# Five feature pairs of the last layer computed with seven half-width block products, and 1 + exp moved to ACT

## The chip, the core and the metric

The kernel runs on one core of a Trainium2 chip. The metric is the device time of one execution in microseconds (us). A core has TensorE (PE in the profile: matrix products; PEld is its loading of the stationary operand), VectorE (DVE), ScalarE (ACT), GpSimd (POOL) and SyncE (SP, which here issues the loads and stores). Each engine works through its own queue in order and waits for the others by semaphores.

## What is computed

The reference is attention over a window of 128 tokens plus 4 sinks, then a gated layer, then a layer with softplus. Only the last one is touched:

```python
def _moe2_ref(x, w_in, w_out):           # x: 1536 x 512, w_in: 512 x 2048, w_out: 2048 x 512
    h = x @ w_in
    g = np.maximum(h, 0.0) + np.log1p(np.exp(-np.abs(h)))
    return (g @ w_out).astype(np.float32)
```

## The kernel before

Every number that goes into a product is held as two parts, a rounded one (hi) and the rest (lo). A product of two such numbers is three matmuls, hi by hi, hi by lo and lo by hi; the helper `mm3` (lines 164 to 168) issues them, so nearly every matmul of the profile has line L166, L167 or L168.

The program has attention, two stages of the gated layer, `stage3` (which leaves the layer's input in 4 slots for each chunk of tokens, named y in the profile and `self.x2` in the code) and `stage4`, the last layer. `stage4` runs over 3 chunks `t` of 512 tokens, and in each over 16 feature blocks `f` of 128 features (called features below; features 2p and 2p+1 are pair p). One turn of the loop does this:

- 12 matmuls of 512 columns give `h` of this feature (4 blocks of 128 inputs by three matmuls) in a PSUM tile of tag `S`; there are 4 such tiles.
- `softplus` works in three steps, between which the loop does other things. First step: absolute value (ACT, L704), exp (ACT, L705), 1 + exp (POOL, L706), all into spa and spu. Second: logarithm (ACT, L709, into spl), and three steps of DVE (L711, L714, L717) that build the maximum and a correction and add them to the logarithm. Third: the hi part by a copy (ACT, L720, into gh) and the lo part by a subtraction (DVE, L151, into gl).
- The third step of a feature is issued in the next turn, behind the first step of the next feature (`next(last[2])`).
- "Value products": `outs` multiplies gh and gl of an earlier feature by `w_out`, 4 groups of 3 matmuls of 512 columns, into the four accumulators ox and o (tags X0, X1, PT). `todo` holds the features whose value products are still owed. In turn f those of feature f - 2 are issued, behind `h` of f. A feature takes 24 matmuls in all.

In chunk 0 the loop also decodes the last four blocks of weights on ACT and DVE (lines 193 to 226), and there a scheduler may move instructions. In chunks 1 and 2 (`tc.manual_schedule()`) each engine gets its instructions in the order in which the code is written. `store` copies an accumulator to SBUF and stores it. At the end the value products of three features and the last one stay behind `h`.

Of the kernel before, what the change touches and what calls it, by code (L numbers as in the profile page):

```python
# [9 lines left out]
F32 = mybir.dt.float32  # L10
FR = mybir.dt.float32r
# [25 lines left out]
NC = DM // P  # L37
NF = FF // P
NF2 = FF2 // P
CH = 512  # L40
NCH = NT // CH
MASKED = 8.0e9
SCALE = 0.125

SLOT_X = 0
# [13 lines left out]
    C=(-143.56, -520.69, 38.35, -348.75, -150.48, -361.46), T=(85.26, 85.11, 83.1, 84.82, 88.43, 82.09),  # L59
    P=(-697.11, -455.77, -631.6, -474.64, -647.58, -395.71), PV=(97.88, 94.31, 94.22, 97.88, 97.88, 169.98),  # L60
# [81 lines left out]
class Net:  # L142
# [545 lines left out]
    def softplus(self, pool, ps, f, t, parts=1):  # L688

        nc = self.nc  # L690

        def tl(n, dt=F32, nb=2):
            return pool.tile([P, CH], dt, tag=n, name=f"{n}{t}_{f}", bufs=nb)

        a, u, l = tl("spa"), tl("spu"), tl("spl")
        if (t, f) == (NCH - 1, NF2 - 1):

            g = self.slot(SLOT_AB, "glast")
            gh, gl = g[:, 0, :], g[:, 1, :]
        else:  # L700
            gh, gl = tl("gh", FR, 3), tl("gl", FR, 3)
        cuts = [slice(j * CH // parts, (j + 1) * CH // parts) for j in range(parts)]
        for c in cuts:
            nc.scalar.activation(a[:, c], ps[:, c], AF.Abs)  # L704
            nc.scalar.activation(a[:, c], a[:, c], AF.Exp, scale=-1.0)  # L705
            nc.gpsimd.tensor_scalar(out=u[:, c], in0=a[:, c], scalar1=1.0, scalar2=1.0, op0=ALU.add, op1=ALU.mult)  # L706
        yield
        for c in cuts:
            nc.scalar.activation(l[:, c], u[:, c], AF.Ln)  # L709

            nc.vector.scalar_tensor_tensor(  # L711
                out=u[:, c], in0=u[:, c], scalar=1.0, in1=a[:, c], op0=ALU.subtract, op1=ALU.subtract
            )
            nc.vector.scalar_tensor_tensor(  # L714
                out=u[:, c], in0=ps[:, c], scalar=0.0, in1=u[:, c], op0=ALU.max, op1=ALU.subtract
            )
            nc.vector.tensor_tensor(out=l[:, c], in0=l[:, c], in1=u[:, c], op=ALU.add)  # L717
        yield
        for c in cuts:
            self.last_hi = nc.scalar.copy(gh[:, c], l[:, c])  # L720
            self.lo_dve(gl[:, c], l[:, c], gh[:, c])
        yield gh, gl

    def stage4(self, pool, psum):
        tc, nc = self.tc, self.nc
        acc = {}

        def outs(t, f, g, parts=range(CH // P)):
            if f == 0:
                acc[t] = [psum.tile([P, CH], F32, tag=f"X{i}", name=f"ox{t}_{i}", bufs=1) for i in range(2)]  # L730
                acc[t] += [psum.tile([P, CH], F32, tag="PT", name=f"o{t}_{i}", bufs=2) for i in range(2)]
            wh, wl = self.w4[f]
            for i in parts:
                k = slice(i * P, (i + 1) * P)
                self.mm3(acc[t][i], (g[0][:, k], g[1][:, k]), (wh[:, 1, :], wl[:, 1, :]), f == 0, f == NF2 - 1)

        def store(t, i, queue=nc.sync):
            r = t * CH + i * P
            o = self.slot(SLOT_X + t * NC + i, f"os{t}_{i}", F32)[:, 0, :]
# [4 lines left out]
            queue.dma_start(out=self.out[r : r + P, :], in_=o)  # L744

        todo, last = [], None
        for t in range(NCH):
            with tc.manual_schedule() if t else contextlib.nullcontext():
                for f in range(NF2):
                    if t == 0 and f in (3, 5, 7, 9):  # L750
                        self.w4_unit(12 + (f - 3) // 2, self.last_hi)
                    if (t, f) == (NCH - 1, NF2 // 2) and self.bad is None:
                        self.bad = self.flag_load()
                    wh, wl = self.w4[f]
                    ps = psum.tile([P, CH], F32, tag="S", name=f"h{t}_{f}", bufs=4)
                    for ct in range(NC):
                        k = slice(ct * P, (ct + 1) * P)
                        x = self.x2[t][ct]
                        self.mm3(ps, (wh[:, 0, k], wl[:, 0, k]), (x[:, 0, :], x[:, 1, :]), ct == 0, ct == NC - 1)
                    sp = self.softplus(pool, ps, f, t, 2 if (t, f) == (NCH - 1, NF2 - 1) else 1)  # L760
                    next(sp)
                    if last:
                        todo.append((*last[:2], next(last[2])))
                    next(sp)
                    last = (t, f, sp)
                    if len(todo) > (1 if (t, f) < (NCH - 1, NF2 - 2) else 3):
                        o = todo.pop(0)
                        outs(*o)
                        if o[1] == NF2 - 1:
                            for i in range(CH // P):  # L770
                                store(o[0], i)
                if t == NCH - 1:

                    while len(todo) > 1:
                        outs(*todo.pop(0))
                    before, n = todo.pop(), CH // P
                    outs(*before, parts=[0, 1])
                    g = next(last[2])
                    for i in range(n):
                        outs(t, NF2 - 1, g, parts=[i])  # L780
                        store(t, i, nc.sync if i < 2 else nc.scalar)
                        if i + 2 < n:
                            outs(*before, parts=[i + 2])


    def dense_masks(self, pool):
# [6 lines left out]
        for i in range(QT):  # L793
# [175 lines left out]
```

## Time and profile before

| | us |
|---|---|
| median of 3 runs | 583.76 (583.74 to 584.16) |
| profiled execution | 584.81 |
| its span, first to last instruction | 582.9 |
| share of the span with PE busy | 98% |
| DVE, ACT, POOL | 74%, 60%, 14% |

The profile is of one execution. A matmul's record runs from its start to the modelled end of its last result, and the next one starts earlier, so the pace of matmuls is read from their starts. Idle time of an engine that nobody waits for costs nothing.

### The profile page before, as it was taken

The page shows a single profiled execution, that of the slowest core. Times are in us where ns is not written, and L with a number is a line of the kernel's source. Part 1 is how long each engine was busy: PE and PEld are TensorE (multiplying, and loading weights), DVE is VectorE, ACT ScalarE, POOL GpSimd, SP SyncE. Part 2 cuts the span into 40 slices and gives each one's busy share as a digit, 9 for nine tenths or more (in the row PEclk, how much of TensorE's full clock was granted, in tenths as well). Part 3 has the DMA queues.
Part 4 walks back from the last instruction along what each step waited for, and adds up shares of the span by engine and source line. Part 5 has one row for each costly group of instructions (what it writes and reads, how often), then busy time and mean ns, then how long its engine had stood idle before and what let it go on. Part 6 is the DMA issues. An engine that isn't in the chain of part 4 may idle for free.

```text
span 582.9 us, 9844 instructions
## 1 busy us (share of the span) xinstructions
PE 573.5 (98%) x3718; PEld 472.8 (81%) x3718; DVE 431.0 (74%) x906; ACT 347.1 (60%) x712; POOL 82.4 (14%) x162
## 2 busy tenths in 40 slices
PE   9999999999999999999999999999999999999996
PEld 6888788888888888888888777888888888888885
DVE  6889899999989976767988889845644554654553
ACT  7999967667566754545666668544444344444352
POOL 4657700000000000000000221111111011011010
PEclk9999999999999999999999999999999999999999
DMA  7566645454445523342643221000200000200002
GB/s 275 172 221 195 188 140 149 139 151 151 133 144 148 164 88 108 114 140 72 201 128 106 74 72 37 0 1 0 73 0 2 0 1 1 73 0 1 0 1 79
DMA packets 15512, 54.51 MB, mean 94 GB/s; under 512 B 1888, under 2 KB 1888, under 8 KB 15456
## 3 DMA queue, kind: packets, MB, share of 16 engines
q1 hardware_dynamic: 15168, 53.27, 29.3%
q8 instruction: 31, 0.51, 0.4%
q10 hardware_dynamic: 288, 0.52, 0.3%
q14 instruction: 25, 0.20, 0.1%
HBM read 50.64 MB, written 3.15 MB: 92 GB/s over the span
## 4 chain that ended last, share of the span: by engine, by line
PE 86%; POOL 4%; DVE 3%; ACT 3%; issue 2%; DMA 1%; SPq 0%; POOLq 0%; DVEq 0%
PE ab L166 8%; PE ab L168 7%; PE ab L167 7%; PE h L167 6%; PE h L168 6%; PE h L166 6%; PE x2p L168 4%; PE x2p L166 4%; PE x2p L167 4%; PE ox L168 3%; PE o L167 3%; PE o L168 3%; PE o L166 3%; PE ox L167 3%; PE ox L166 3%; PE w34p L168 2%
## 5 line engine op out<-in xcount | busy, mean ns | idle before, releaser
L706 POOL TENSOR_SCALAR spu<-spa 128x512 f32<-128x512 f32 (+1 forms) x49 | 35.9, 733 | 458.7 <-ACT spa L705 458.7
L151 DVE TENSOR_TENSOR gl<-spl,gh 128x512 fp32r<-128x512 f32 x47 | 32.6, 694 | 76.8 <-ACT gh L720 76.5
L704 ACT ACTIVATE spa<-h 128x512 f32<-128x512 f32 (+1 forms) x49 | 28.7, 586 | 86.5 <-PE h L168 86.3
L166 PE MATMUL ab<-x,u_w 128*128 128x512 f32 x192 | 74.8, 390 | 0.0
L167 PE MATMUL ab<-x,u_w 128*128 128x512 f32 x192 | 74.7, 389 | 0.0
L168 PE MATMUL ab<-x,u_w 128*128 128x512 f32 x192 | 74.7, 389 | 0.0
L166 PE MATMUL h<-y,w4h 128*128 128x512 f32 x192 | 74.7, 389 | 0.0
L167 PE MATMUL h<-y,w4h 128*128 128x512 f32 x192 | 74.7, 389 | 0.0
L168 PE MATMUL h<-y,w4l 128*128 128x512 f32 x192 | 74.7, 389 | 0.0
L193 ACT ACTIVATE dt_w<-raw_w 128x512 bf16<-128x512 bf16 x64 | 42.5, 669 | 52.1 <-DMA raw_w<-w4d 16.9
L201 DVE SCALAR_TENSOR_TENSOR dc_w<-raw_w,dt_w 128x512 uint16<-128x512 uint16 x64 | 44.2, 697 | 10.1 <-ACT dt_w L196 9.6
L196 ACT ACTIVATE dt_w<-dt_w,rebias 128x512 uint16<-128x512 uint16 x64 | 45.8, 721 | 1.3
L711 DVE SCALAR_TENSOR_TENSOR spu<-spu,spa 128x512 f32<-128x512 f32 (+1 forms) x49 | 33.3, 680 | 16.6 <-ACT spl L709 16.6
L709 ACT ACTIVATE spl<-spu 128x512 f32<-128x512 f32 (+1 forms) x49 | 30.4, 623 | 24.5 <-POOL spu L706 24.5
L407 POOL TENSOR_SCALAR e<-e,st 128x196 f32<-128x196 f32 (+1 forms) x96 | 39.5, 434 | 23.4 <-ACT e L393 17.1
L393 ACT ACTIVATE e<-e,st 128x196 f32<-128x196 f32 (+1 forms) x96 | 42.2, 447 | 0.9 <-DVE st L386 0.7
L168 PEld LDWEIGHTS ab<-x,u_w 128*128 128x128 f32 x192 | 36.1, 188 | 7.5
L167 PEld LDWEIGHTS h<-y,w4h 128*128 128x128 f32 x192 | 36.1, 188 | 7.5
L167 PEld LDWEIGHTS ab<-x,u_w 128*128 128x128 f32 x192 | 36.0, 188 | 7.5
L166 PEld LDWEIGHTS h<-y,w4h 128*128 128x128 f32 x192 | 36.0, 188 | 7.5
L166 PEld LDWEIGHTS ab<-x,u_w 128*128 128x128 f32 x192 | 36.0, 188 | 7.4
L168 PEld LDWEIGHTS h<-y,w4l 128*128 128x128 f32 x192 | 36.0, 188 | 7.4
(127 smaller groups left out, 1306.4 us busy)
## 6 DMA issues: line engine op xcount, KB each, us to landing
raw_w<-w4d SPq DMA_DIRECT2D x32, 511.8 KB, 4.2
raw_w<-w SPq DMA_DIRECT2D x16, 511.8 KB, 4.6
raw_w<-w3t SPq DMA_DIRECT2D x16, 511.8 KB, 3.8
qk<-qk SPq DMA_DIRECT2D x7, 792.0 KB, 4.5
raw_wo<-wod SPq DMA_DIRECT2D x8, 511.8 KB, 3.8
v<-vu SPq DMA_DIRECT2D x8, 400.0 KB, 5.5
v<-v SPq DMA_DIRECT2D x8, 384.0 KB, 4.6
out<-os SPq DMA_DIRECT2D x10, 256.0 KB, 2.3
```

Source lines behind the costliest of these rows:

```text
L151: return engine.tensor_tensor(out=lo, in0=x, in1=hi.bitcast(F32), op=ALU.subtract)
L166: nc.tensor.matmul(ps, lhs[0], rhs[0], start=start, stop=False)
L167: nc.tensor.matmul(ps, lhs[0], rhs[1], start=False, stop=False)
L168: nc.tensor.matmul(ps, lhs[1], rhs[0], start=False, stop=stop)
L193: return nc.scalar.activation(t.bitcast(BF), x["top"].bitcast(BF), AF.Abs)
L196: return nc.scalar.activation(x["t"], x["t"], AF.Relu, bias=self.rebias[:, 0:1], scale=8.0)
L201: nc.vector.scalar_tensor_tensor(out=c, in0=x["top"], scalar=0x8000, in1=t, op0=ALU.bitwise_and, op1=ALU.bitwise_or)
L393: nc.scalar.activation(e, e, AF.Exp, bias=st[:, 0, i : i + 1], scale=-1.0, accum_out=st[:, 1, i : i + 1])
L407: nc.gpsimd.tensor_scalar(out=e, in0=e, scalar1=buf("st", h)[:, 2, i : i + 1], scalar2=1.0, op0=ALU.mult, op1=ALU.mult)
L706: nc.gpsimd.tensor_scalar(out=u[:, c], in0=a[:, c], scalar1=1.0, scalar2=1.0, op0=ALU.add, op1=ALU.mult)
L709: nc.scalar.activation(l[:, c], u[:, c], AF.Ln)
L711: nc.vector.scalar_tensor_tensor(out=u[:, c], in0=u[:, c], scalar=1.0, in1=a[:, c], op0=ALU.subtract, op1=ALU.subtract)
```

## The change

For pairs 3, 5 and 7 of chunk 1 and pairs 3 and 5 of chunk 2, `h` of the two features is no longer 24 matmuls of 512 columns. The pair is taken as a 2 x 2 by 2 x 2 block product (2 features by 2 halves of the inputs, times 2 halves of the inputs by 2 halves of the tokens), and that is formed from seven block products of sums, each of 6 matmuls of 256 columns: 42 matmuls in place of 24.

The sums are made on DVE ahead of time and split into hi and lo: for the weights once for each pair (`weight_steps`, issued in feature 2p - 2, tiles wr and ws), for the tokens twice for each chunk (`token_steps`, tiles xr and ts: in features 14 of chunk 0 and 2 of chunk 1, and in 0 and 2 of chunk 2). In `seven` DVE then adds the products into a tile `hp` in SBUF, from which `softplus` reads both features at once. The value products of the two features before the pair are cut in their 8 groups: one behind the second product, four between the sixth (the fourth of the tiles A, Bk, C, E) and the last, three behind that.

The second edit is in `softplus`: 1 + exp is an Identity with a bias on ACT. Its bias is a second column of the tile `rebias`, which gets a second memset. Chunk 0 stores through two slots in place of four.

```diff
@@ softplus
-            nc.gpsimd.tensor_scalar(out=u[:, c], in0=a[:, c], scalar1=1.0, scalar2=1.0, op0=ALU.add, op1=ALU.mult)
+            nc.scalar.activation(u[:, c], a[:, c], AF.Identity, bias=self.one[:, 0:1])
@@ stage4
+        def whole(r, hi, lo):
+            nc.vector.tensor_tensor(out=r, in0=hi.bitcast(F32), in1=lo.bitcast(F32), op=ALU.add)
+        def combine(out, x, y, op):
+            nc.vector.tensor_tensor(out=out, in0=x, in1=y, op=op)
...
+        def parts_of(r, dst):
+            for j in range(2):
+                nc.scalar.copy(dst[j][:, 0, :], r[j])
+            yield
+            for j in range(2):
+                self.lo_dve(dst[j][:, 1, :], r[j], dst[j][:, 0, :])
+            yield
...
+        def weight_steps(t, p):
+            r = pair_of_r(f"wr{t}_{p}")
+            for dst, f in zip(r, (2 * p + 1, 2 * p)):
+                hi, lo = self.w4[f]
+                whole(dst, hi[:, 0, :], lo[:, 0, :])
+            a11, a12, a21, a22 = r[0][:, HN], r[0][:, HM], r[1][:, HN], r[1][:, HM]
+            combine(a22, a21, a22, ALU.add)
+            combine(a21, a11, a21, ALU.subtract)
+            combine(a11, a22, a11, ALU.subtract)
+            combine(a12, a12, a11, ALU.subtract)
+            yield
+            self.ws = [self.slot(SLOT_X + j, f"ws{t}_{p}_{j}") for j in range(2)]
+            yield from parts_of(r, self.ws)
+        def product(ps, a, b, start=True):
+            for c in range(2):
+                self.mm3(ps, a(c), b(c), start and c == 0, c == 1, skip_group_check=True)
...
+            product(A[:, HN], part(odd, 0), tok(0, HN))
+            p1 = quarter("dt", "p1")
+            nc.scalar.copy(p1, A[:, HN])
+            before()
+            chunks = [lambda o=o, i=i: outs(*o, parts=[i]) for o in todo for i in range(CH // P)]
+            product(Bk[:, HN], part(even, 2), tsum(1, HN))
+            chunks[0]()
+            product(A[:, HN], part(odd, 2), tok(2, HN), False)
+            nc.scalar.copy(ho[:, HN], A[:, HN])
+            product(Bk[:, HM], wsum(0, 0), tsum(1, HM))
+            u2 = quarter("dc", "u2")
+            combine(u2, Bk[:, HM], p1, ALU.add)
+            product(C[:, HN], wsum(1, 0), tsum(0, HN))
+            u3 = quarter("dt", "u3")
+            combine(u3, C[:, HN], u2, ALU.add)
+            combine(he[:, HN], u3, Bk[:, HN], ALU.subtract)
+            product(E[:, HN], wsum(1, 2), tsum(0, HN))
+            combine(he[:, HM], E[:, HN], u3, ALU.add)
+            for c in chunks[1:5]:
+                c()
+            product(E[:, HN], wsum(0, 2), tok(2, HM), False)
+            combine(ho[:, HM], E[:, HN], u2, ALU.add)
+            for c in chunks[5:]:
+                c()
+            e = self.softplus(pool, he, 2 * p, t)
...
+        lots = {1: (3, 5, 7), 2: (3, 5)}
@@ the loop, around softplus of a plain feature
+                    sums = steps.get((t, f), iter(lambda: 0, 1))
+                    next(sums)
                     sp = self.softplus(pool, ps, f, t, 2 if (t, f) == (NCH - 1, NF2 - 1) else 1)
                     next(sp)
+                    next(sums)
                     if last:
                         todo.append((*last[:2], next(last[2])))
                     next(sp)
+                    next(sums)
```

The order is shown at two places of chunk 1: between pairs 3 and 5 on DVE and ACT, and at the start of pair 5 on PE. Names end in chunk and feature: h1_8 is `h` of feature 8 in chunk 1; the long numbers are buffers, and each version has its own line numbers.

**First place.** DVE before, from the end of feature 7 to that of feature 8:

```order
L717 TENSOR_TENSOR spl1_7_4771<-spl1_7_4771,spu1_7_4770 128x512
L151 TENSOR_TENSOR gl1_7_4773<-spl1_7_4771,gh1_7_4772 128x512
L711 SCALAR_TENSOR_TENSOR spu1_8_4809<-spu1_8_4809,spa1_8_4808 128x512
L714 SCALAR_TENSOR_TENSOR spu1_8_4809<-h1_8_4795,spu1_8_4809 128x512
L717 TENSOR_TENSOR spl1_8_4810<-spl1_8_4810,spu1_8_4809 128x512
L151 TENSOR_TENSOR gl1_8_4812<-spl1_8_4810,gh1_8_4811 128x512
```

The lo part of feature 7 is followed at once by the three steps of feature 8.

DVE after, the same stretch; wr are the sums of the weights of pair 5 and ws their two parts:

```order
L152 TENSOR_TENSOR gl1_7_4857<-spl1_7_4855,gh1_7_4856 128x512
L753 TENSOR_TENSOR wr1_5_0_4882<-w4h11_3744,w4l11_3745 128x512
L753 TENSOR_TENSOR wr1_5_1_4883<-w4h10_3740,w4l10_3741 128x512
L756 TENSOR_TENSOR wr1_5_1_4883<-wr1_5_1_4883 128x256
L756 TENSOR_TENSOR wr1_5_1_4883<-wr1_5_0_4882,wr1_5_1_4883 128x256
L756 TENSOR_TENSOR wr1_5_0_4882<-wr1_5_1_4883,wr1_5_0_4882 128x256
L756 TENSOR_TENSOR wr1_5_0_4882<-wr1_5_0_4882 128x256
L712 SCALAR_TENSOR_TENSOR spu1_8_4891<-spu1_8_4891,spa1_8_4890 128x512
L715 SCALAR_TENSOR_TENSOR spu1_8_4891<-h1_8_4869,spu1_8_4891 128x512
L718 TENSOR_TENSOR spl1_8_4892<-spl1_8_4892,spu1_8_4891 128x512
L152 TENSOR_TENSOR ws1_5_0_4898<-wr1_5_0_4882,ws1_5_0_4898 128x512
L152 TENSOR_TENSOR ws1_5_1_4899<-wr1_5_1_4883,ws1_5_1_4899 128x512
```

The next row is `gl1_8_4894`. So eight instructions came in: six sums between features 7 and 8, and two rests ahead of the lo part of feature 8.

ACT before, from the logarithm of feature 7 to the hi part of feature 8:

```order
L709 ACTIVATE spl1_7_4771<-spu1_7_4770 128x512
L704 ACTIVATE spa1_8_4808<-h1_8_4795 128x512
L705 ACTIVATE spa1_8_4808<-spa1_8_4808 128x512
L720 CAST gh1_7_4772<-spl1_7_4771 128x512
L709 ACTIVATE spl1_8_4810<-spu1_8_4809 128x512
L704 ACTIVATE spa1_9_4847<-h1_9_4834 128x512
L705 ACTIVATE spa1_9_4847<-spa1_9_4847 128x512
L720 CAST gh1_8_4811<-spl1_8_4810 128x512
```

The logarithm of feature 8 waits for POOL and stands behind two copies and activations of features 7 and 8 alone.

ACT after, the same stretch:

```order
L710 ACTIVATE spl1_7_4855<-spu1_7_4854 128x512
L721 CAST gh1_7_4856<-spl1_7_4855 128x512
L705 ACTIVATE spa1_8_4890<-h1_8_4869 128x512
L706 ACTIVATE spa1_8_4890<-spa1_8_4890 128x512
L707 ACTIVATE spu1_8_4891<-spa1_8_4890,rebias_60 128x512
L773 CAST ws1_5_0_4898<-wr1_5_0_4882 128x512
L773 CAST ws1_5_1_4899<-wr1_5_1_4883 128x512
L710 ACTIVATE spl1_8_4892<-spu1_8_4891 128x512
L705 ACTIVATE spa1_9_4933<-h1_9_4920 128x512
L706 ACTIVATE spa1_9_4933<-spa1_9_4933 128x512
L707 ACTIVATE spu1_9_4934<-spa1_9_4933,rebias_60 128x512
L721 CAST gh1_8_4893<-spl1_8_4892 128x512
```

The two copies of the sums stand ahead of the logarithm of feature 8, the hi part of feature 7 ahead of feature 8's absolute value, and 1 + exp is new.

**Second place.** PE before, the end of `h` of feature 10 and the first value products of feature 8:

```order
L166 MATMUL h1_10_4873<-y1_3_3512,w4h10_3739 128x512
L167 MATMUL h1_10_4873<-y1_3_3512,w4h10_3739 128x512
L168 MATMUL h1_10_4873<-y1_3_3512,w4l10_3740 128x512
L166 MATMUL ox1_0_4584<-w4h8_3731,gh1_8_4811 128x512
L167 MATMUL ox1_0_4584<-w4l8_3732,gh1_8_4811 128x512
L168 MATMUL ox1_0_4584<-w4h8_3731,gl1_8_4812 128x512
```

All 12 matmuls of feature 10 stand ahead of the value products of feature 8.

PE after, from the middle of the second product of pair 5:

```order
L167 MATMUL q1_5_1_4960<-ts1_1_1_4600,w4h10_3740 128x256
L168 MATMUL q1_5_1_4960<-ts1_1_1_4600,w4h10_3740 128x256
L169 MATMUL q1_5_1_4960<-ts1_1_1_4600,w4l10_3741 128x256
L167 MATMUL ox1_0_4611<-w4h8_3732,gh1_8_4893 128x512
L168 MATMUL ox1_0_4611<-w4l8_3733,gh1_8_4893 128x512
L169 MATMUL ox1_0_4611<-w4h8_3732,gl1_8_4894 128x512
```

Between the value products of feature 7 and the first of feature 8 stood 12 matmuls of 512 columns; now 12 of 256 stand there.

## Rows read from the trace of the kernel before

**Rows 1.** The page's head: span, busy time (share) xinstructions, clock in 40 slices.

```profile
span 582.9 us, 9844 instructions
PE 573.5 (98%) x3718; PEld 472.8 (81%) x3718; DVE 431.0 (74%) x906; ACT 347.1 (60%) x712; POOL 82.4 (14%) x162
PEclk9999999999999999999999999999999999999999
```

**Rows 2.** Stretches of the last layer: us, busy of each engine (xinstructions), clock, DMA.

```profile
314.00:397.00 83.00, 81.90 (x355) 65.91 (x354) 65.18 (x104) 50.46 (x88) 15.06 (x15) 1.00 0.10 33
397.00:482.00 85.00, 85.00 (x376) 70.41 (x375) 44.97 (x66) 37.67 (x64) 9.87 (x16) 1.00 0.04 13
```

**Rows 3.** Timeline of PE in chunk 2: start us, us, engine, line, operation, xcount.

```profile
487.01 0.39 PE L166 MATMUL h<-y,w4h 128*128 128x512 f32 x1
487.23 0.39 PE L167 MATMUL h<-y,w4h 128*128 128x512 f32 x1
...
487.69 0.39 PE L166 MATMUL ox<-w4h,gh 128*128 128x512 f32 x1
...
488.37 0.39 PE L166 MATMUL ox<-w4h,gh 128*128 128x512 f32 x1
```

**Rows 4.** Timeline, a feature's softplus in chunk 2; in brackets idle before, and releaser.

```profile
487.89 0.60 ACT L704 ACTIVATE spa<-h 128x512 f32<-128x512 f32 x1 [2.81 <-PE h L168]
488.52 0.63 ACT L705 ACTIVATE spa<-spa 128x512 f32<-128x512 f32 x1
...
490.55 0.69 DVE L711 SCALAR_TENSOR_TENSOR spu<-spu,spa 128x512 f32<-128x512 f32 x1 [0.16 <-ACT spl L709]
491.27 0.69 DVE L714 SCALAR_TENSOR_TENSOR spu<-h,spu 128x512 f32<-128x512 f32 x1
492.00 0.69 DVE L717 TENSOR_TENSOR spl<-spl,spu 128x512 f32<-128x512 f32 x1
...
494.49 0.60 ACT L720 CAST gh<-spl 128x512 fp32r<-128x512 f32 x1
495.13 0.70 DVE L151 TENSOR_TENSOR gl<-spl,gh 128x512 fp32r<-128x512 f32 x1 [2.44 <-ACT gh L720]
```

**Rows 5.** Timeline of chunk 0 around one instruction of POOL.

```profile
341.44 1.29 DVE L210 SCALAR_TENSOR_TENSOR dr_w<-raw_w,dt_w 128x512 f32<-128x512 uint32 x2
...
341.96 3.05 POOL L706 TENSOR_SCALAR spu<-spa 128x512 f32<-128x512 f32 x1 [5.72 <-ACT spa L705]
...
344.21 0.39 PE L167 MATMUL ox<-w4l,gh 128*128 128x512 f32 x1
344.59 0.50 PE L168 MATMUL ox<-w4h,gl 128*128 128x512 f32 x1
344.93 0.39 PE L166 MATMUL ox<-w4h,gh 128*128 128x512 f32 x1
...
345.05 0.63 ACT L709 ACTIVATE spl<-spu 128x512 f32<-128x512 f32 x1 [3.17 <-POOL spu L706]
```

**Rows 6.** POOL by line, in chunk 0 and in chunks 1 and 2.

```profile
L706 POOL TENSOR_SCALAR spu<-spa 128x512 f32<-128x512 f32 x15 | 15.1, 1004 | 303.3 <-ACT spa L705 303.3
L706 POOL TENSOR_SCALAR spu<-spa 128x512 f32<-128x512 f32 (+1 forms) x34 | 20.9, 614 | 155.4 <-ACT spa L705 155.4
```

**Rows 7.** Loads of weights in chunk 1, by line: busy us, mean ns.

```profile
L167 PEld LDWEIGHTS h<-y,w4h 128*128 128x128 f32 x64 | 12.0, 188 | 2.5
```

**Rows 8.** Timeline of PE in attention: short matmuls with a new weight each.

```profile
14.68 1.08 PE L420 MATMUL pt<-ident,e 128*68 128x128 f32 x8
```

**Rows 9.** DVE by line, 512 columns in chunks 1 and 2, 256 at the end.

```profile
L717 DVE TENSOR_TENSOR spl<-spl,spu 128x512 f32<-128x512 f32 x31 | 21.5, 693 | 1.1
...
L717 DVE TENSOR_TENSOR spl<-spl,spu 128x256 f32<-128x256 f32 x2 | 0.8, 424 | 0.1
```

**Rows 10.** ACT by line: plain and with a bias tile, 512 columns.

```profile
L705 ACT ACTIVATE spa<-spa 128x512 f32<-128x512 f32 x32 | 20.2, 632 | 1.0
L720 ACT CAST gh<-spl 128x512 fp32r<-128x512 f32 x31 | 18.7, 604 | 0.0
...
L196 ACT ACTIVATE dt_w<-dt_w,rebias 128x512 uint16<-128x512 uint16 x8 | 5.3, 707 | 0.0
```

**Rows 11.** DVE by line in attention, 256 columns with one input in PSUM.

```profile
L151 DVE TENSOR_TENSOR x<-xt,x 128x256 fp32r<-128x256 f32 x9 | 3.5, 408 | 0.0
```

More of the change, by code (lines that the diff above doesn't have):

```diff
@@ L41 @@
 NCH = NT // CH
+HN, HM = slice(0, CH // 2), slice(CH // 2, CH)
 MASKED = 8.0e9
@@ new lines, in pair_of_r, with token_steps @@
+        def pair_of_r(name):
+            return [self.dec.tile([P, CH], F32, tag="dr", name=f"{name}_{j}", bufs=2) for j in range(2)]
+        def parts_of(r, dst):
[5 more added lines that the diff above has]
+            yield
+        def token_steps(t, c):
+            r = pair_of_r(f"xr{t}_{c}")
+            token_sums(t, c, r)
+            yield
+            for j in range(2):
+                name = f"ts{t}_{c}_{j}"
+                if (c, j) == (1, 1):
+                    self.ts[c, j] = self.slot(SLOT_X + 3, name)
+                else:
+                    self.ts[c, j] = self.dec.tile([P, 2, CH], FR, tag="raw", name=name, bufs=3)
+            yield from parts_of(r, [self.ts[c, j] for j in range(2)])
@@ new lines, in product, with seven, part, tok @@
+        def product(ps, a, b, start=True):
+            for c in range(2):
+                self.mm3(ps, a(c), b(c), start and c == 0, c == 1, skip_group_check=True)
+        def seven(t, p, before, todo):
+            odd, even, x = self.w4[2 * p + 1], self.w4[2 * p], self.x2[t]
+            def part(pair, c0):
+                return lambda c: tuple(w[:, 0, (c0 + c) * P : (c0 + c + 1) * P] for w in pair)
+            def tok(c0, cols):
+                return lambda c: tuple(x[c0 + c][:, j, cols] for j in range(2))
+            def wsum(j, c0):
+                return lambda c: tuple(self.ws[j][:, k, (c0 + c) * P : (c0 + c + 1) * P] for k in range(2))
+            def tsum(j, cols):
+                return lambda c: tuple(self.ts[c, j][:, k, cols] for k in range(2))
+            def quarter(tag, n):
+                return self.dec.tile([P, CH // 2], F32, tag=tag, name=f"{n}_{t}_{p}", bufs=2)
+            A, Bk, C, E = [psum.tile([P, CH], F32, tag="S", name=f"q{t}_{p}_{j}", bufs=4) for j in range(4)]
+            h = self.slot(SLOT_X + 2, f"hp{t}_{p}", F32)
+            he, ho = h[:, 0, :], h[:, 1, :]
+            product(A[:, HN], part(odd, 0), tok(0, HN))
[10 more added lines that the diff above has]
+            combine(u2, Bk[:, HM], p1, ALU.add)
+            product(C[:, HN], wsum(1, 0), tsum(0, HM))
+            u3 = quarter("dt", "u3")
[10 more added lines that the diff above has]
+            e = self.softplus(pool, he, 2 * p, t)
+            next(e)
+            next(e)
+            o = self.softplus(pool, ho, 2 * p + 1, t)
+            next(o)
+            g = next(e)
+            next(o)
+            return [(t, 2 * p, g), (t, 2 * p + 1, next(o))]
@@ L746, in stage4 @@
+        self.ts, steps = {}, {}
+        lots = {1: (3, 5, 7), 2: (3, 5)}
+        steps[0, NF2 - 2], steps[1, 2] = token_steps(1, 0), token_steps(1, 1)
+        steps[2, 0], steps[2, 2] = token_steps(2, 0), token_steps(2, 1)
+        for t, lot in lots.items():
+            for p in lot:
+                steps[t, 2 * p - 2] = weight_steps(t, p)
         todo, last = [], None
         for t in range(NCH):
+            pairs = lots.get(t, ())
             with tc.manual_schedule() if t else contextlib.nullcontext():
@@ L753, in stage4, with before @@
                         self.bad = self.flag_load()
+                    if f // 2 in pairs:
+                        if f % 2 == 0:
+                            def before():
+                                todo.append((*last[:2], next(last[2])))
+                            todo = seven(t, f // 2, before, todo)
+                            last = None
+                        continue
                     wh, wl = self.w4[f]
@@ L911, in run @@
             self.val = const.tile([P, 2], F32, name="val")
-            self.rebias = const.tile([P, 1], F32, name="rebias")
+            both = const.tile([P, 2], F32, name="rebias")
+            self.rebias, self.one = both[:, 0:1], both[:, 1:2]
             self.idle = const.tile([P, P], BF, name="idle")
@@ L915, in run @@
             nc.vector.memset(self.rebias, -8.0 * 16 * 896)
+            nc.vector.memset(self.one, 1.0)
             nc.scalar.preload_act_table_set("natural_log_exp_and_others")
```

25 lines of the change are left out of this document (20 added, 5 removed).

## The prediction

> **What bounds the kernel now.** I read the page's head first: PE is busy for 98% of the span at the full granted clock, its 2.4 GHz level [rows 1]. So only what shortens or stops PE's stream counts. Then the stretches of the last layer and the starts of matmuls in it: six intervals take 488.37 - 487.01 = 1.36 us, 0.2267 each [rows 3]. In chunk 1, 376 matmuls at that pace are 85.2 us for a stretch of 85.0: PE never waits. In chunk 0, 355 are 80.5 of 83.0: 2.5 us are lost, which the busy column hides, since records overlap [rows 2] (a few records may be missing, so this is no better than to 0.5).
>
> Where they are lost shows the timeline of chunk 0: POOL's 1 + exp takes 3.05 us from 341.96, while DVE works without a pause; the logarithm has to wait for it until 345.05 [rows 5]. By line POOL's step means 1.00 us in chunk 0 and 0.61 later [rows 6]. DVE is behind by then, and PE stops for gl. A late weight also costs a restart: the matmul at 344.59 lasts 0.50 in place of 0.39 and the next starts 0.34 later, 0.11 over the pace.
>
> Last, one feature of chunk 2: the steps of ACT and DVE, with ACT idle 2.81 and DVE 2.44 in a turn of 5.44 [rows 4]. `h` of this feature ends at 487.69, gl at 495.83, and its value products come four half turns after `h`, at 498.57: 2.7 us to spare. That slack must carry the sums.
>
> **The change, part by part.**
>
> *The products.* A pair had 24 matmuls at 0.2267, 5.44 us; it gets 42 of 256 columns, whose pace the trace does not show. Bounds: half of 0.2267 is 0.113; a load of weights is on record for 0.188 [rows 7], and if it could not lie under the matmul before, that would be the pace. Loads need not be alone: eight matmuls of 128 columns with a new weight each take 1.08 us, 0.28 of it the last one's own record, so 0.114 each [rows 8]; and the restart above costs 0.11, not 0.188. At 2.4 GHz one column a cycle is 213 ns for 512, which leaves 13 per matmul; 107 + 13 = 0.120 is my value. 42 x 0.120 = 5.04, 0.40 less; five pairs: **-2.0 us** (-3.4 at 0.113, +12.3 at 0.188; even at 0.130).
>
> The Trainium skill (TensorE: Matmul & The Clock Gate, Back-to-back issue gap) gives columns over 2.4 GHz and 2.5 ns, 0.216 at 512, where the row has 0.227. By it the 256 columns would pass in 0.109 and the products alone bring -4.3 us. Which end is nearer decides one of the rivals below.
>
> *1 + exp.* POOL's step goes, and with it the waits of chunk 0 except some 0.4 at its start: **-2.1 us** (0 to -2.5). ACT takes over 16 steps there, 11 us on top of 50.5 in 83 [rows 2]; this fits. A step is 0.63 without a bias tile and 0.707 with one [rows 10]; the edit has one, so I take 0.707. In chunks 1 and 2 it replaces 0.62 and two handovers, so nobody gains. The memset is once, at the start, beside loads; the stores of chunk 0 keep their times.
>
> *The sums and the chain behind them.* Prices: a DVE step of 512 is 0.69, of 256 columns 0.42 [rows 9] (0.41 with an input in PSUM [rows 11]). If it needs the result just before, the next starts 0.035 later [rows 4], if not, 0.08 sooner: two take 1.29 [rows 5]. The sums of a pair are 0.61 + 0.73 + 4 x 0.46 = 3.17 us of DVE, two copies 1.1 of ACT, two rests 1.2 of DVE. Averaged over two pairs (21 us) DVE has room: 4 features x 2.8 + 3.2 + 1.2 + five sums in the pair 2.2 = 17.8. What matters is that the order is fixed. The order rows show the sums between gl of feature 7 and the first step of feature 8, the copies ahead of its logarithm, the rests ahead of its gl. So feature 8 waits for all that.
>
> The place is pair 5 of chunk 1. Let Z be the moment when PE leaves the seventh product of pair 3. PE then has three value groups (2.04), `h` of 8, value products of 6, `h` of 9, value products of 7 (2.72 each) and two products (1.44): it wants gh of feature 8 at **Z + 14.4**. Before, with a whole `h` in place of the two products, that was 2.72 - 1.44 = 1.3 later.
>
> DVE and ACT meanwhile, both features of pair 3 being ready almost at once and `softplus` of 7 queued behind that of 6. DVE is done with feature 5 some 3.5 before Z, four sums of products (0.46 each) end at Z - 1.7, four steps of ACT for feature 6 (0.64, 0.67, 0.74, 0.67) bring the logarithm at Z + 0.9. Then there is no pause: three DVE steps (0.73 each) to 3.1, gh 0.64 to 3.7, gl 0.61, three steps for feature 7 to 6.5, gh to 7.15, gl to 7.8, the sums 3.17 to 10.9, two copies 1.05 to 12.0, logarithm 0.66 to 12.6, three steps to 14.8, gh to 15.4, and with handover and restart (0.15) PE goes on at **Z + 15.6**. It waits 1.2. After two matmuls it wants gl; that stands behind the two rests, begins at 15.95, ends at 16.65 and restarts PE at 16.8, another 0.75. Together 2.0.
>
> The same reckoning elsewhere, each with its own start:
> - pair 7 of chunk 1 and pair 5 of chunk 2 lie alike, 2.2 each: the first begins with DVE already late, in the second ACT reads the flag of the window first;
> - pair 3, twice: sums start when DVE is through with feature 3, 0.8 after `h` of 4; 3.2 more, two copies 1.05 and gh 0.6 make 5.7 with the restart, against 5.44; gl 0.27 later. 0.5 each;
> - features 14 and 15 of chunk 1, computed at once by pair 7: 1.0;
> - sums of tokens in feature 2, twice, behind the copies to be stored: 0.3 each.
>
> Sum 2.0 + 2.2 + 2.2 + 1.0 + 1.0 + 0.6 = **+9.0 us**. Bounds: if a sum of 256 columns took 0.38, the waits would lose 2, at 0.46 they gain 2; handovers of 0.06 in place of 0.035 add 3. Without the bias tile (0.63) they lose 0.6.
>
> The Trainium skill (ScalarE: Activation LUTs, What ACT_TABLE_LOAD costs) prices an activation of 512 columns at 0.61 with an immediate bias and 0.71 with a tile's. The trace has 0.63 and 0.707: it agrees on the second. Taken at 0.61 the sum would come out 0.8 lower.
>
> Sum: -2.0 - 2.1 + 9.0 = **+4.9 us**. The profiled execution of 584.81 (582.9 span and 1.9 around it) would be 589.7. It lies 1.05 over the median of 583.76, and 583.76 + 4.9 = 588.7 is the forecast.
>
> **The rivals.**
>
> *The sums stay hidden* (the other side). Mechanism: the chain between pairs 3 and 5 ends before PE asks. It is 14.7 us from Z + 0.9 against 13.5 that PE leaves. The waits fall below the 4.1 that the rest brings when it shrinks by about 1 us, 7%. For: DVE is idle for half of chunk 1 [rows 2], and nobody saw these sums of 256 columns in such a row. Against: each step has a row of its shape. Largely hidden, the waits are 1: -2.0 - 2.1 + 1.0 = -3.1, 580.7.
>
> *The load of weights is the pace.* 0.188 per product [rows 7]: 5 x 42 x 0.068 = 14.3 more on PE. The slower products give the chain more time, 4 of the waits go: 4.9 + 14.3 - 4 = +15, 599. Against: rows 8 and the restart of 0.11. It outweighs the forecast from 0.14 on.
>
> *The edit of 1 + exp frees nothing in chunk 0.* ACT, first in the chain there, takes 0.71 for POOL's 0.62 and has the decoding to do; if the waits stay, +4.9 + 2.1 = +7.0, 590.8.
>
> *A quicker product.* If all of a matmul's time goes with its columns, 256 pass in 0.113, 5 x 42 x 0.007 = 1.5 less on PE. At the four places where the chain of DVE ends last PE only waits longer; about 0.2 remains, 588.5. The gap rule of the Trainium skill named above lies at this end: 0.109, and some 0.4 off the time.
>
> **Chances and range.** Forecast 0.66, quick product 0.08, no gain in chunk 0 0.10, load-bound 0.06, hidden 0.10, of which 0.08 end below -0.2% and 0.02 near no change; 0.02 more of the forecast's own lower tail fall within. A measurement of this kernel tells 0.2%, 1.2 us, from no change. So faster 0.08, same 0.04, slower 0.88. The range takes the prices of the sums (+2.0 to +8.5): 585.9 to 592.3. It leaves out the load-bound case, the hidden one and a few hundredths at both ends.
>
> **What would show it.** Right: starts of 256-column matmuls 0.12 apart; PE's waits for gh (ACT) and gl (DVE) in chunks 1 and 2, most by the value products of features 8 and 12, some 9 us, none such before; chunk 0 without waits beyond its start; POOL idle there. Wrong: starts 0.15 or more apart; no waits at features 8 and 12, which would say that DVE's small sums are cheaper than their rows or run ahead; or waits at the combining sums, inside a pair, which I take to be covered by the value groups.

## The result, and the profile after

| | before | after | ratio, 95% interval |
|---|---|---|---|
| first comparison, median of 4 and 4 runs | 583.96 us | 590.98 us (590.52 to 591.28) | 1.0111 (1.0090 to 1.0132) |
| second comparison, median of 23 and 4 runs | 584.48 us | 591.25 us (590.17 to 591.77) | 1.0104 (1.0082 to 1.0127) |

The changed kernel is 7 us slower. The forecast was 588.7, in a range from 585.9 to 592.3: the sign and the range held, the size was 2 us short. (In the diff above one operand is misprinted: the product into C reads `tsum(0, HM)`. And in ACT's order before, one copy stands ahead of the logarithm of feature 8, not two.)

The page's head of the profiled execution after, to be read beside [rows 1]: span, busy time (share) xinstructions, clock.

```profile
span 589.1 us, 10106 instructions
PE 575.8 (98%) x3808; PEld 476.7 (81%) x3808; DVE 471.4 (80%) x1004; ACT 393.6 (67%) x789; POOL 46.4 (8%) x113
PEclk9999999999999999999999999999999989999999
```

PE's busy column says 98% again and hides the loss. DVE has 40 us more to do, ACT 46, POOL 36 less, and one slice of PEclk has an 8. The same stretches as in [rows 2]:

```profile
314.00:397.00 83.00, 83.00 (x367) 68.32 (x366) 67.90 (x114) 64.41 (x107) 0.00 (x0) 1.00 0.11 33
397.00:482.00 85.00, 81.99 (x404) 68.45 (x403) 62.35 (x107) 50.54 (x87) 0.00 (x0) 0.98 0.04 13
```

In chunk 0 PE is now busy all the time (367 matmuls for 355); in chunk 1 it stands still for 3 of 85 us, which it never did before. The starts of matmuls on PE's timeline, at the first value products of feature 8, show where:

```profile
451.89 0.28 PE L168 MATMUL q<-ts,w4h 128*128 128x256 f32 x1
452.01 0.28 PE L169 MATMUL q<-ts,w4l 128*128 128x256 f32 x1
453.21 0.51 PE L167 MATMUL ox<-w4h,gh 128*128 128x512 f32 x1 [0.91 <-ACT gh L721]
453.55 0.39 PE L168 MATMUL ox<-w4l,gh 128*128 128x512 f32 x1
454.36 0.50 PE L169 MATMUL ox<-w4h,gl 128*128 128x512 f32 x1 [0.42 <-DVE gl L152]
454.70 0.28 PE L167 MATMUL q<-y,w4h 128*128 128x256 f32 x1
```

The matmuls of 256 columns start 0.12 apart, as taken in the prediction. Then gh is late, and after two matmuls gl. DVE and ACT in the row that makes them late (timeline; in brackets the idle time before, and what ended it):

```profile
444.88 0.69 DVE L152 TENSOR_TENSOR gl<-spl,gh 128x512 fp32r<-128x512 f32 x1 [0.74 <-ACT gh L721]
445.49 1.29 DVE L753 TENSOR_TENSOR wr<-w4h,w4l 128x512 f32<-128x512 f32 x2
446.81 0.43 DVE L756 TENSOR_TENSOR wr<-wr 128x256 f32<-128x256 f32 x1
...
450.36 0.69 DVE L712 SCALAR_TENSOR_TENSOR spu<-spu,spa 128x512 f32<-128x512 f32 x1 [1.74 <-ACT spl L710]
...
452.42 1.29 DVE L152 TENSOR_TENSOR ws<-wr,ws 128x512 fp32r<-128x512 f32 x2
453.62 0.69 DVE L152 TENSOR_TENSOR gl<-spl,gh 128x512 fp32r<-128x512 f32 x1
```

```profile
448.65 1.14 ACT L773 CAST ws<-wr 128x512 fp32r<-128x512 f32 x2 [1.88 <-DVE wr L756]
449.70 0.62 ACT L710 ACTIVATE spl<-spu 128x512 f32<-128x512 f32 x1
...
452.54 0.62 ACT L721 CAST gh<-spl 128x512 fp32r<-128x512 f32 x1 [0.30 <-DVE spl L718]
```

Engines take turns without slack: sums, copies (ACT had been idle for 1.88), logarithm, DVE's three steps (DVE had been idle for 1.74), gh; then gl behind the two rests. The logarithm's own input was there at 446.77, when ACT's 1 + exp ended; it begins at 449.70, since the order puts the copies, which wait for the sums, ahead of it.

**The account of the last layer.** "Lost" is what an interval between two starts exceeds 0.227 (512 columns) or 0.120 (256) by, where that is over 0.06. "After" was profiled twice (the second trace is the run a2 below).

| place | predicted | after | after, second trace |
|---|---|---|---|
| chunk 0 | 0.4 | 0.2 | 0.2 |
| features 0 and 1 of chunks 1 and 2 (sums of tokens) | 0.6 | 0.4 | 0.4 |
| pair 3, twice | 1.0 | 1.0 | 0.9 |
| pair 5, chunk 1 | 2.0 | 1.9 | 1.9 |
| pair 7, chunk 1 | 2.2 | 2.2 | 2.2 |
| feature 14, chunk 1 | 1.0 | 0 | 0.9 |
| pair 5, chunk 2 | 2.2 | 2.0 | 1.9 |
| products at half the clock | - | 1.4 | 0 |
| the last feature | - | 0.1 | 0.1 |

Without chunk 0, the products at half the clock and the last feature, the chain of sums costs 7.5 in the first trace and 8.4 in the second, for 9.0 predicted; the first lacks the wait for feature 14. What remains to be explained is why the gains on the other side were smaller.

### The profile page after: what moved, and what is told of

Its sections match the earlier page's. It is cut to its first block, busy times and chain, and to the rows that moved or that the text cites. A ratio compares the mean times of both kernels' runs of the same rounds, so it can differ in the third digit from the quotient of the medians.

```text
span 589.1 us, 10106 instructions
## 1 busy us (share of the span) xinstructions
PE 575.8 (98%) x3808; PEld 476.7 (81%) x3808; DVE 471.4 (80%) x1004; ACT 393.6 (67%) x789; POOL 46.4 (8%) x113
## 4 chain that ended last, share of the span: by engine, by line
PE 73%; DVE 15%; ACT 7%; POOL 3%; issue 1%; DVEq 0%; POOLq 0%; ACTq 0%
PE ab L167 7%; PE ab L169 7%; PE ab L168 7%; PE h L169 4%; PE x2p L167 4%; PE h L168 4%; PE x2p L168 4%; PE x2p L169 4%; PE h L167 4%; PE w34p L169 2%; PE w34p L167 2%; DVE gl L152 2%; PE w34p L168 2%; POOL e L408 2%; PE pt L421 2%; PE xt L457 2%
## 5 line engine op out<-in xcount | busy, mean ns | idle before, releaser
L167 PE MATMUL h<-y,w4h 128*128 128x512 f32 x152 | 59.2, 389 | 0.0
L169 PE MATMUL h<-y,w4l 128*128 128x512 f32 x152 | 59.2, 389 | 0.0
L168 PE MATMUL h<-y,w4h 128*128 128x512 f32 x152 | 59.2, 389 | 0.0
L721 ACT CAST gh<-spl 128x512 fp32r<-128x512 f32 x47 | 28.9, 614 | 32.7 <-DVE spl L718 32.7
L167 PE MATMUL ox<-w4h,gh 128*128 128x512 f32 x94 | 37.6, 400 | 3.2 <-ACT gh L721 3.2
L705 ACT ACTIVATE spa<-h 128x512 f32<-128x512 f32 (+1 forms) x39 | 22.7, 581 | 24.7 <-PE h L169 24.7
L169 PE MATMUL ox<-w4h,gl 128*128 128x512 f32 x94 | 37.5, 399 | 1.3 <-DVE gl L152 1.3
L168 PE MATMUL x2p<-ab,w 128*128 128x512 f32 x96 | 37.4, 389 | 0.0
L169 PE MATMUL x2p<-ab,w 128*128 128x512 f32 x96 | 37.4, 389 | 0.0
```

The source lines that it names most:

```text
L169: nc.tensor.matmul(ps, lhs[1], rhs[0], start=False, stop=stop, **kw)
```

## The experiments

### The parts alone

**e1: 1 + exp on ACT, and nothing else.**

```diff
-            nc.gpsimd.tensor_scalar(out=u[:, c], in0=a[:, c], scalar1=1.0, scalar2=1.0, op0=ALU.add, op1=ALU.mult)
+            nc.scalar.activation(u[:, c], a[:, c], AF.Identity, bias=self.one[:, 0:1])
```

> The kernel before with 1 + exp on ACT alone; no sums, no products of blocks. Theory (the sums' place in the fixed order of DVE and ACT is what costs): this edit only gains, it takes away the stops of PE in chunk 0, 2.1 us of 583.96, so 581.9, ratio 0.9964, and PE has no new waits in chunks 1 and 2. Rival A (ACT, 393.6 us busy in the changed kernel and 347.1 before, is what makes gh late): PE waits for gh here too, 584 or more. Rival B (the edit frees nothing): 584.0, with the wait at the logarithm of chunk 0 still there.

Measured: 585.39 (12 runs) against 584.24 (23 runs), ratio 1.0013 (1.0002 to 1.0024). The theory's 581.9 fell: the edit gains no time, as rival B has it, and the time is even 1.15 us over before, a difference that just clears the noise and whose cause stays open. Yet the trace shows what the theory wanted: PE loses 0.55 in the whole last layer for 2.64 in the trace of before, no wait for the logarithm, and none of rival A's waits for gh. A gain of 2 us that one trace against another shows and the times do not: this made the next question whether the stop in [rows 5] belongs to the kernel at all.

**e2: the products, with 1 + exp left on POOL.**

```diff
-            nc.scalar.activation(u[:, c], a[:, c], AF.Identity, bias=self.one[:, 0:1])
+            nc.gpsimd.tensor_scalar(out=u[:, c], in0=a[:, c], scalar1=1.0, scalar2=1.0, op0=ALU.add, op1=ALU.mult)
```

> The changed kernel with 1 + exp back on POOL. Theory (the sums): PE's stops in chunk 0 come back, 2.3 us; at features 8 and 12 the chain holds the same steps, with 0.62 on POOL and two handovers for 0.71 on ACT, so the waits there stay at 1.9 to 2.2 each: 593.3, ratio to before 1.016. Rival A (ACT's extra work makes the waits): they shrink to under 1 each and the time is 589 or less. Rival C (POOL's step is held up beside the two-input sums of DVE as it is in chunk 0, 3.05 us): waits of 4 to 5 at features 8 and 12, 600 or more.

Measured: 595.14, ratio 1.0190 (1.0172 to 1.0208); about 4 us over the changed kernel, more than the theory's 2.3, under rival C's. And by another way: chunk 0, where POOL, DVE and ACT have the same order as before (up to the sums of tokens at 368 us), lost only 0.5. The loss stands in chunks 1 and 2: 2.7 at pair 5 for 1.9, pair 3 twice 0.9 for 0.5, feature 14 1.1. PE's waits, and POOL and DVE at feature 8:

```profile
PE ox L167 <- ACT gh L721: 5.9, 6, 1.8
```

```profile
447.26 1.16 POOL L707 TENSOR_SCALAR spu<-spa 128x512 f32<-128x512 f32 x1 [5.93 <-ACT spa L706]
...
447.97 0.72 DVE L756 TENSOR_TENSOR wr<-wr 128x256 f32<-128x256 f32 x1
```

POOL's step takes 1.16 for 0.62 and DVE's sum 0.72 for 0.42: beside the sums the two hold each other up. In this trace 1.5 us more are products at half the clock (last section). So 1 + exp on ACT is worth nothing by itself and 4 us to this change; against the trace a2 below, some 2.5 of them are waits and 1.5 the slow products.

**e3: no sums of weights.**

```diff
-                return lambda c: tuple(self.ws[j][:, k, (c0 + c) * P : (c0 + c + 1) * P] for k in range(2))
+                return lambda c: tuple(w[:, 0, (c0 + c) * P : (c0 + c + 1) * P] for w in (odd, even)[j])
...
-                steps[t, 2 * p - 2] = weight_steps(t, p)
+                pass
```

> The changed kernel without the sums of weights, their copies and their rests: the products that need a sum of weights read a plain weight of the same pair in its place. All 3808 matmuls, the sums of tokens and the combining sums stay. Left out: 30 sums, 10 copies and 10 rests in five features. Theory (the sums): the waits at pairs 3, 5 and 7 (8.5 us with the stretch of slow products at 479.03 that follows them) go, the products keep their 0.12: 591.0 - 8.5 = 582.5 or less, down to 580.5; ratio to before 0.994 to 0.998. Rival D (the 90 added matmuls, or the place of the value products, make the loss): 589 to 591. Rival E (the combining sums inside a pair hold PE up): waits at the products that read the next bank stay, and half of the loss with them, about 587.

Measured: 583.51, ratio 0.9991 (0.9979 to 1.0002); D and E fall. PE at the place that cost 1.9 us:

```profile
452.50 0.28 PE L169 MATMUL q<-ts,w4l 128*128 128x256 f32 x1
452.62 0.40 PE L167 MATMUL ox<-w4h,gh 128*128 128x512 f32 x1
452.86 0.40 PE L168 MATMUL ox<-w4l,gh 128*128 128x512 f32 x1
453.09 0.39 PE L169 MATMUL ox<-w4h,gl 128*128 128x512 f32 x1
```

The layer loses 0.8 in all. This removes the whole loss of the change, so its cause is shown: the sums of weights, with their copies and rests, in this row of DVE and ACT. Their shares are not parted by e3; x1 and x2 below change the rests and the sums by themselves, and the copies alone were not tried. It also bounds what these five pairs could bring: with the sums of weights for nothing the kernel is 0.1% faster than before, at most 0.2%. That is 1 us short of the theory's upper end (582.5) and 3 of its lower: the other terms, too, give less than they should.

**p1: the sums of weights on POOL.**

```diff
-                whole(dst, hi[:, 0, :], lo[:, 0, :])
+                nc.gpsimd.tensor_tensor(out=dst, in0=hi[:, 0, :].bitcast(F32), in1=lo[:, 0, :].bitcast(F32), op=ALU.add)
...
-            combine(a22, a21, a22, ALU.add)
+            nc.gpsimd.tensor_tensor(out=a22, in0=a21, in1=a22, op=ALU.add)
```

(and the three other sums alike)

> The changed kernel with the six sums of weights of each pair on POOL in place of DVE; copies stay on ACT, rests on DVE. Theory (the sums): what makes PE wait is 3.2 us of DVE in the row between gl of feature 2p-1 and the steps of feature 2p-2; on POOL, idle there, they can begin much sooner, since they read weights alone, and the chain loses 3.2 us: the waits of 1.9 to 2.2 go, 583 to 584, ratio 0.998 to 1.001. Rival C (POOL comes to nothing while DVE works without a pause, as in chunk 0 where a step of 0.62 took 3.05): the copies wait for POOL, PE for the copies, 591 or more.

Measured: 597.21, ratio 1.0223 (1.0207 to 1.0239). The theory fell. The time is rival C's, its mechanism only in part. POOL's 512-column sums in chunks 1 and 2 (busy us, mean ns), who waited for whom there (us, times, longest), then a stretch of POOL and DVE:

```profile
L795 POOL TENSOR_TENSOR wr<-w4h,w4l 128x512 f32<-128x512 f32 x10 | 16.5, 1666 | 423.2 <-ACT gh L721 423.2
```

```profile
ACT ws L773 <- POOL wr L800: 5.3, 2, 2.7
PE q L167 <- DVE hp L756: 3.6, 4, 1.1
PE ox L169 <- DVE gl L152: 3.1, 5, 1.4
```

```profile
456.14 3.28 POOL L795 TENSOR_TENSOR wr<-w4h,w4l 128x512 f32<-128x512 f32 x2 [17.67 <-ACT gh L721]
...
456.51 1.76 DVE L152 TENSOR_TENSOR gl<-spl,gh 128x512 fp32r<-128x512 f32 x1
...
458.19 1.77 DVE L712 SCALAR_TENSOR_TENSOR spu<-spu,spa 128x512 f32<-128x512 f32 x1
```

A sum of 512 takes POOL 1.67 for DVE's 0.68, and while it runs DVE's gl takes 1.76 in place of 0.69. The copies wait for POOL, as rival C has it, at pair 3 alone (twice); at the other pairs the sums are ready in time, and what PE waits for is DVE, held up beside POOL. PE now waits inside the pairs as well (1.3 lost at a combining sum). The Trainium skill (SBUF — State Buffer, Who interferes with whom) says that a VectorE instruction with two inputs in SBUF contends with a GpSimd instruction that reads SBUF, that the port which they share is an exclusive lock, and that the order of issue decides who blocks. These rows agree: gl begins 0.38 after POOL's first sum and lasts 1.07 longer than alone.

### Is the stop in chunk 0 the kernel's?

**b2 and b3: the kernel before, unchanged, for two more traces.**

> The kernel before, unchanged, for a second trace of it and for what two runs of one kernel differ by. Theory A (the stop of PE in chunk 0, 2.6 us, belongs to the kernel, by POOL's place in the fixed order): POOL's step of 3.05 and the waits for gl and gh at 344 to 357 stand here again, within 0.5 us. Theory B (it belongs to the one execution that was profiled, since the kernel with the products alone has the same order of ACT, DVE and POOL there and lost 0.46 in chunk 0): waits under 1 us in chunk 0 and no POOL step over 1.3. Ratio 1.000 +- 0.001 in both.

> The kernel before once more, for its trace alone. Theory A: 2.6 us lost in chunk 0 again. Theory B: under 1 us; if it is large in one of the two traces and small in the other, the stop comes in some executions and not in others.

Measured: b2 584.06 against 584.48, ratio 0.9999 (0.9985 to 1.0013); b3 585.1, one run. POOL by line in chunk 0, b2 and b3, beside the 15.1 and 1004 of [rows 6]:

```profile
L706 POOL TENSOR_SCALAR spu<-spa 128x512 f32<-128x512 f32 x16 | 10.1, 631 | 311.5 <-ACT spa L705 311.5
```

```profile
L706 POOL TENSOR_SCALAR spu<-spa 128x512 f32<-128x512 f32 x16 | 10.2, 635 | 311.6 <-ACT spa L705 311.6
```

And b2's timeline at the place of [rows 5]:

```profile
341.25 1.71 DVE L210 SCALAR_TENSOR_TENSOR dr_w<-raw_w,dt_w 128x512 f32<-128x512 uint32 x2
...
341.72 0.70 POOL L706 TENSOR_SCALAR spu<-spa 128x512 f32<-128x512 f32 x1 [5.31 <-ACT spa L705]
...
342.45 0.63 ACT L709 ACTIVATE spl<-spu 128x512 f32<-128x512 f32 x1 [0.81 <-POOL spu L706]
```

Theory B holds. The same two engines meet at the same instruction, but here DVE stands back (1.71 for two steps that took 1.29) and POOL is through in 0.70; in the first trace POOL stood back, behind four instructions of DVE, for 3.05. Chunk 0 lost 0.45 and 0.46 for 2.64, and the last layer from its first matmul to the last took 261.41 and 261.39 for 263.65. So the stop came in one of three traces of before, and e2, with the same order there, did not have it either.

**a2: the changed kernel, a second trace.**

> The changed kernel, unchanged, for a second trace. Theory (the waits come from the fixed order of the sums): the waits of pairs 3, 5 and 7 stand at the same products with the same sizes within 0.3 us each (1.9, 2.2, 2.0 and twice 0.5). Rival (they are an accident of one execution, as the stop of before in chunk 0 may be): other places or sizes. The stretch at half the clock, 1.5 us after the wait for feature 12: stands here again if the wait brings it, else not. Ratio to before 1.010 to 1.013.

Measured: 591.25, ratio 1.0104; the waits stand at the same products with the same sizes (table above), so they are the order's and no accident. Only the stretch at half the clock is missing, and with it the wait for feature 14 is there that the first trace had not:

```profile
454.65 0.50 PE L167 MATMUL ox<-w4h,gh 128*128 128x512 f32 x1 [0.93 <-ACT gh L721]
...
455.81 0.50 PE L169 MATMUL ox<-w4h,gl 128*128 128x512 f32 x1 [0.43 <-DVE gl L152]
...
491.42 0.50 PE L167 MATMUL ox<-w4h,gh 128*128 128x512 f32 x1 [0.36 <-ACT gh L721]
```

### How the row of the sums acts

**s1: three pairs, none close behind another.**

```diff
-        lots = {1: (3, 5, 7), 2: (3, 5)}
+        lots = {1: (3, 7), 2: (5,)}
```

> The changed kernel with three pairs in place of five and none two pairs behind another in a chunk: pairs 3 and 7 in chunk 1, pair 5 in chunk 2. Theory (a pair's sums cost most where the softplus of the pair before still queues on DVE): each pair waits as pair 3 did, 0.5, in place of 2.0; of the changed kernel's 591.0 go two pairs' waits and the slow stretch, 8.6 - 1.5 = 7.1, and 0.8 comes back for the products: 584.7, ratio to before 1.000 to 1.002. Rival (the sums of any pair cost the same wherever it stands, 1.7 with the slow stretch shared out): 591.0 - 3.4 + 0.8 = 588.4, ratio 1.007.

Measured: 584.52, ratio 1.0000 (0.9989 to 1.0011). The theory gave 584.7, the rival 588.4. Pair 3 loses 0.4, pair 7 at the value products of feature 12 nothing (2.2 when pair 5 stood ahead of it), feature 14 behind it 0.4, and pair 5 of chunk 2, alone in its chunk, nothing. PE at the value products of feature 14, with starts 0.32 to 0.39 apart and no idle time that the view shows:

```profile
485.75 0.48 PE L167 MATMUL ox<-w4h,gh 128*128 128x512 f32 x1
486.07 0.39 PE L168 MATMUL ox<-w4l,gh 128*128 128x512 f32 x1
486.46 0.50 PE L169 MATMUL ox<-w4h,gl 128*128 128x512 f32 x1
```

**x1: the rests of the sums left out.**

```diff
-            yield from parts_of(r, self.ws)
+            for j in range(2):
+                nc.scalar.copy(self.ws[j][:, 0, :], r[j])
+            yield
+            yield
```

> The changed kernel without the rests of the sums of weights: two DVE steps of 0.64 fewer in each of five pairs; the products take the plain weights' second part in their place. Theory (the order of DVE: the rests stand between the steps of feature 2p-2 and its gl): the wait for gl at features 8, 12 and 8, 0.60 each, falls to the 0.16 that a wait for gl has anywhere; the wait for gh ahead of it, which ends before the rests begin, stays at 1.1 to 1.4; in all 1.4 to 2.5 less, 588.5 to 589.8. Rival (PE waits since DVE is short on average): the wait for gh shrinks by the 1.2 of DVE that the pair before no longer needs, and most of the loss goes, 585.

Measured: 589.74, ratio 1.0075 (1.0047 to 1.0103). At feature 8 the interval ahead of the matmul with gl shrinks from 0.81 to 0.39, as the order says, the wait for gh from 0.91 to 0.63:

```profile
453.60 0.50 PE L167 MATMUL ox<-w4h,gh 128*128 128x512 f32 x1 [0.63 <-ACT gh L721]
453.94 0.40 PE L168 MATMUL ox<-w4l,gh 128*128 128x512 f32 x1
454.33 0.50 PE L169 MATMUL ox<-w4h,gl 128*128 128x512 f32 x1
```

Feature 12 then loses 2.0 at gh where it had lost 1.4: PE arrives sooner, DVE's row ends no sooner. The theory's total was right, the rival's 585 falls; the single waits for gh did not stay where the theory had them, and 0.9 of this trace is products of 256 columns at half the clock.

**x2: the four sums of 256 columns made twice.**

```diff
             combine(a12, a12, a11, ALU.subtract)
+            combine(a22, a21, a22, ALU.add)
+            combine(a21, a11, a21, ALU.subtract)
+            combine(a11, a22, a11, ALU.subtract)
+            combine(a12, a12, a11, ALU.subtract)
```

> The changed kernel with the four sums of 256 columns of each pair of weights made twice, the second time of the results: 4 x 0.46 = 1.84 of DVE more in each of five pairs. Theory (this row of DVE is the path from the end of one pair to the features ahead of the next): each of the five waits for gh grows by the whole 1.84, 9.2 in all, or 1.6 where a restart was paid already: 599 to 601, ratio to before 1.025 to 1.028. Rival (the row is covered in part, and the copies or the clock set the wait): under half of that, 595 or less.

Measured: the profiled run 600.26, inside the 599 to 601 expected, the median of four 602.97, over it; ratio 1.0325 (1.0288 to 1.0362). For 1.84 us more of DVE the four places at pairs 3 and 5 lose 1.7 more each, pair 7 1.1:

```profile
457.09 0.50 PE L167 MATMUL ox<-w4h,gh 128*128 128x512 f32 x1 [2.64 <-ACT gh L721]
```

7.9 in all for the 9.2 expected, plus 1.4 of products at half the clock: the row has no cover worth the name. Why the other three runs were still longer, the last section says as far as it is known.

## Why the prediction was right or wrong

**The sums (+9.0): right, place by place; 8.4 in the second trace.** With Z the end of pair 3's seventh product (437.75 in the trace after), the working and the trace stand like this:

| | predicted | trace |
|---|---|---|
| PE wants gh of feature 8 | Z + 14.4 | Z + 14.38 |
| the sums end | 10.9 | 10.87 |
| copies end | 12.0 | 12.04 |
| logarithm ends | 12.6 | 12.57 |
| gh ends | 15.4 | 15.41 |
| PE goes on | 15.6 | 15.46 |
| gl starts | 15.95 | 15.87 |
| PE goes on behind gl | 16.8 | 16.61 |

Nothing in it needed a new price: 0.69, 0.42, 0.035 between dependent steps [rows 4, 9] and the order gave it. e3 took the row away and the loss went; x2 lengthened it and the loss grew by nearly as much; s1 moved pairs apart and most of it went. The waits at the combining sums inside a pair, which would have proved it wrong, did not come.

**The pace of 256 columns (0.120): right, the gain from it half gone.** 210 of them pass in 25.1 us, 0.1194 each, for 27.2 of the 120 that they replace: -2.1 for the -2.0 predicted. What was not in the sum: the 512-column matmuls beside them pass in 0.2275 on average, for 0.2267 in b2. Behind a run of short ones, or a restart, some six start about 0.232 apart. Over 1031 matmuls that is +0.8. The rivals on the pace (0.188, and 0.113 with the 0.109 at its end) are out.

**1 + exp (-2.1): wrong.** This is the step that failed; the runs show -0.2 in its place. It took the stop of POOL in [rows 5] and [rows 6] for the kernel's; b2, b3 and e2 show that it was that one execution's. Against a trace of before without it the edit brings 0.2 in chunk 0, and the whole layer of e1 is 0.35 longer than b2's (261.76). The prediction had the warning in its own text, that the profiled execution lay 1.05 over the median, and nevertheless took 2.1 off the median for a stop which the median run need not have. The rival "The edit of 1 + exp frees nothing in chunk 0" gave 590.8 and the time came out at 591.0, but its mechanism (the waits stay, since ACT is no faster than POOL) is not what happened: the waits were gone, and were mostly not there before.

**The sum, redone** from b2 (261.41) to a2 (268.36): products -2.1, slower neighbours +0.8, waits 8.70 - 0.45 = +8.25, together +6.95, which is the difference of the two layers (6.95), and of the medians (7.0 and 6.8). By the first pair of traces the layer grew by only 5.2, close to the predicted 4.9, for the wrong reason.

**Feature 14 (1.0): right in the second trace.** In the first the slow products of pair 7 cost 1.4 and gave the chain that time, so that the wait vanished; x1, with slow products at the same place, does not have it either.

A version that beats before was not found: s1 is equal to it, and e3, which no longer pays for the sums of weights, bounds what a better place for them can bring. An order in which the copies stand behind the logarithm, which had its input 2.9 us before it began, was not tried.

## What to carry to other kernels

A wait in one profile is a fact about one execution. Before its removal is booked as a gain, see whether the profiled run lies over the median by about as much, and look at a second trace, or at another kernel with the same order there. Where two engines wait for each other in a fixed order, average room on an engine says nothing: write the row out step by step from its instructions' durations, and every microsecond put ahead of the step that PE waits for is paid nearly whole once there is no slack (in x2 1.7 of 1.84 at four places, 1.1 at the fifth). The same work spread so that each row keeps its slack costs little, but then the gain, here 0.4 us a pair, has to be worth more than what it loosens elsewhere.

## What the runs showed of the hardware that was not expected

**The granted clock.** Behind the waits for feature 12 (PE idle for 1.25 and 0.42 us) the profiled run of after has products of 256 columns that start 0.213 apart in place of 0.120. Stretches before, in and after it: us, busy time of each engine (xinstructions), granted clock, DMA:

```profile
475.00:479.00 4.00, 2.33 (x14) 1.64 (x14) 3.97 (x7) 2.22 (x5) 0.00 (x0) 1.00 0.00 0
479.10:482.40 3.30, 3.30 (x17) 3.30 (x17) 3.27 (x8) 0.89 (x2) 0.00 (x0) 0.50 0.00 0
482.50:490.00 7.50, 7.50 (x38) 6.35 (x38) 4.24 (x10) 4.86 (x8) 0.00 (x0) 1.00 0.00 0
```

It is at the 1.2 GHz level there and at 2.4 on both sides. In a2 the same waits are not followed by a fall; x1 has one behind the wait for feature 12, e2 and x2 behind that for feature 8, p1 none with more idle time in all. So such a wait can bring slow products of 1.4 or 1.5 us with it in some executions; in the trace after 0.9 of it came back, since the wait for feature 14 went. The four runs of x2 fit this: mean granted clocks of 0.994, 0.994, 0.987 and 0.983 with 600.26, 602.08, 603.86 and 605.37 us. That the longer ones had more such stretches was not seen, since only the first left a trace.

**Who stands back.** POOL and DVE met at the same instruction in [rows 5] and in b2; in one POOL waited for four of DVE's instructions in a row, in the other DVE waited 0.4 for POOL. The first trace of before has such a step once more, at a place where PE lost nothing, and a later one of the same kind that was through at once:

```profile
329.53 3.12 POOL L706 TENSOR_SCALAR spu<-spa 128x512 f32<-128x512 f32 x1 [5.30 <-ACT spa L705]
...
354.31 0.64 POOL L706 TENSOR_SCALAR spu<-spa 128x512 f32<-128x512 f32 x1 [5.72 <-ACT spa L705]
```

POOL's record begins ahead of DVE's next one by 0.15 and 0.08 at the two that stood back, and by 0.08 at the one that did not, so that the lead does not tell which. What decides it stays open; by these records the order of issue, named at p1, does not account for it.

**Runs of one program differ by 3 us** (before: 583.4 to 586.7 in one comparison), and not only in such stops: the first matmul of the last layer starts at 313.57, 314.69 and 315.13 in the three traces of before, and the time from the start of the last matmul to the end is 5.64, 5.83 and 6.48. A gain of 1 us is not to be had from two traces.
